# The written-out order of the first units and of the last stores in a fused HGRN2 and bilinear-FFN kernel

## The chip, the cores and the metric

The kernel runs on one core of a Trainium2 chip. The metric is the device time of one execution in microseconds (us). Three executions of the kernel before took 578.60, 579.79 and 579.91 us; the median is 579.79.

## The reference

The first stage is a gated linear attention (HGRN2 with outer products), the second a bilinear feed-forward network on its output:

```python
# q, k, v, f_logit: (B=4, H=8, S=768, D=48), fp32
f = 1.0 / (1.0 + np.exp(-f_logit))
for t in range(S):
    state = f[:, :, t, :, None] * state + np.einsum('bhd,bhe->bhde', k[:, :, t], v[:, :, t])
    y[:, :, t] = np.einsum('bhd,bhde->bhe', q[:, :, t], state)
x = y.transpose(0, 2, 1, 3).reshape(B * S, H * D)          # 3072 x 384
out = ((x @ w_a) * (x @ w_b)) @ w_out                      # 384 -> 1536 -> 384
```

The three weights are float64 in device memory and are turned into fp32 on the chip.

## The kernel before, in words

`by_quotients` is the main path. It cuts the attention into 16 units: unit u is one batch entry, one half of the sequence (384 tokens) and four heads. Two units give the 384 columns of x for a block of 384 tokens, so there are 8 blocks. Three sets of buffers hold the inputs of the units in turn. A unit goes through these stages, named as in the code:

- `front_parts`, in four parts of up to three steps. Part 0 is the sigmoid of the logits and two more steps on ScalarE (ACT). Part 1 on VectorE (DVE) holds two running products along the sequence (`scan_f`) and a third step, `hold`, which compares and counts for a test at the end. Part 2 restarts the products at the boundaries of small chunks and takes their inverse. Part 3 multiplies k (first step) and q (second step) by them.
- `turn` transposes k on TensorE (PE), `turned` copies the result (kT) out of PSUM on ACT, `scores` multiplies k and q within a chunk of 64 tokens (L426), `mask` applies the causal pattern on DVE (L443), `gains` forms the state products of v and kT (L506), `carried` sums the states on DVE.
- `within` multiplies the masked scores by v (L566), `across` the states by q (L592), both into the unit's PSUM bank. `y_of` copies it to SBUF on ACT (L610) and stores it to xT (L632).

The FFN of a block follows: `up` (L676 for the first block), `product`, `down`. Weights arrive in 12 pieces of 768 KB. `load_weights` issues the next piece on SyncE (SP), L275; `begin(n)` and `end(n)` emit the first and the last part of the conversion of the pieces up to n (half steps such as 2.5 emit half of a begin), on ACT, DVE and GpSimd (POOL).

For the first four units the order of all engines' work is written out by hand, as a list of calls that starts at L1202; each engine does its instructions in the order in which the list emits them. Later units are placed by a planner, whose rules stay as they are. The list has three calls of `keep_up` (L1190): products of the identity and a buffer of running products into an idle PSUM bank, which nobody reads. The names `idle[-1]` and `ps_f_68` stand for such a bank; the buffer, `products_of_f`, is part of the tile `groups`.

At the end a number (`bad`) that the kernel has computed decides over a branch. One arm computes everything again in another way; the other, short one does what the list `ending` holds. `down_thirds` (L981) is the last block's second FFN matmul by a scheme with few products: it makes sums of products in the PSUM banks v, u, r, t, and `c` holds the block's result, in three block rows of two halves. `add` and `add_steps` are DVE sums (L795), `store` is an output DMA (L1028). Every engine reads `bad` and goes over the branch (L142).

Of the kernel before, what the change touches and what calls it, by code (L numbers as in the profile page):

```python
# [22 lines left out]
BLK = 384  # L23
# [130 lines left out]
def by_quotients(ctx, tc, q, k, f_logit, v, moe_w_a, moe_w_b, moe_w_out, out, ident, weights, bad, ps_f):  # L154
# [64 lines left out]
    def load_unit(u, names="fkqv"):  # L219
        for do in loads_of(u, names):  # L220
            do()
# [40 lines left out]
    def load_weights(n=1):  # L262
        for _ in range(n):
            if len(raws) == len(todo):
                return
            dst, src, (k, m) = todo[len(raws)]
            raw = dst
            if src.dtype != FP32:

                if len(raws) in EARLY:  # L270
                    raw = groups[:, EARLY.index(len(raws))].bitcast(mybir.dt.uint64)
                else:
                    raw = next(raw_places)
                raw = raw[:, 0:k * m].rearrange("p (k m) -> p k m", k=k)
            nc.sync.dma_start(out=raw, in_=src)  # L275
            raws.append(raw)

    def begin(n):

        while 2 * n > begun[0] < 2 * len(todo):  # L280
            i, second = divmod(begun[0], 2)
            dst, src, shape = todo[i]
            if not second:
                going.append(
                    from_double(
                        nc, dst, raws[i], shape[0], next(blocks), bits[i % len(bits)], some, whole, shape[0] == NKT
                    )
                    if src.dtype != FP32 else iter(())
                )
            next(going[i], None)  # L290
            begun[0] += 1
# [126 lines left out]
    def scores(u):  # L418
        t = sets[u % NSET]
        qf, kf = halves(t["q"]), halves(t["k"])  # L420
        ps = pair_of(home(u))
        for n, c, o in each():
            for h in range(2):
                for p in range(2):
                    r = slice(R * h, R * h + D)
                    nc.tensor.matmul(  # L426
                        ps[h][SUB * p:SUB * p + SUB, o:o + SUB],
                        lhsT=kf[r, tokens(n, c, p)],
                        rhs=qf[r, tokens(n, c, p)],
                        start=True,  # L430
                        stop=True,
                    )

    def mask(u):

        if u == NQ - 1:

            at = raws4[:, 3 * PIECE:4 * PIECE].bitcast(FP32)[:, 0:2 * BLK].rearrange("s (h t) -> s h t", h=2)
        else:
            at = sb1.tile([128, 2, BLK], FP32, tag="at", name="at")  # L440
        to, x = (y.rearrange("s h (o t) -> s h o t", t=SUB) for y in (at, home(u)[:, :, 0:BLK]))
        tri = causal.unsqueeze(1).unsqueeze(1)
        nc.vector.tensor_tensor(to, x, tri.broadcast_to((128, 2, 2 * NC, SUB)), ALU.mult)  # L443
        live[u]["at"] = at
# [112 lines left out]
    def within(u):  # L557

        t, at = sets[u % NSET], live[u]["at"]
        ps = live[u]["y"] = pair_of(home(u) if u < 2 * NQ else ps_y)  # L560
        for n, c, o in each():
            for p in range(2):
                for h in range(2):
                    r = slice(SUB * p, SUB * p + SUB)
                    e = R * (p ^ h)
                    nc.tensor.matmul(  # L566
                        ps[p][e:e + D, o:o + SUB],
                        lhsT=t["v"][r, n, c, h * D:h * D + D],
                        rhs=at[r, h, o:o + SUB],
                        start=o == 0,  # L570
                        stop=True,
                        skip_group_check=True,
                    )
# [85 lines left out]
    def on(engine, load, due, do, *args, copied=False):  # L659
        return engine + COPIED * copied, load, beats[0] + due if due else 1 << 30, do, *args  # L660
# [325 lines left out]
    def down_thirds(blk, ending=None):  # L986
# [36 lines left out]
        def add(due, k, i, ps):  # L1023
            return on(DVE, 270, due, add_steps, c[:, k, i], c[:, k, i], ps, ALU.subtract if k == 1 else ALU.add)
# [61 lines left out]
        if ending is not None:  # L1086
            yield from times(v, "v6")
            ending.extend((
                (add_steps, c[:, 2, 0], u, c[:, 2, 0]), (store, 2), (write, c[:, 1, 0], v, -1), (store, 1, slice(0, 1)),
            ))  # L1090
            return
        yield add(5, 2, 0, u)
        yield on(SP, ISSUE, 0, store, 2)
        yield from times(v, "v6")
# [77 lines left out]
    with tc.manual_schedule():  # L1172
# [13 lines left out]
        def emit_all(steps):  # L1186
            for _, _, do, *args in steps:
                do(*args)

        def keep_up(n, to):  # L1190

            x = products_of_f[0][:, 0]
            for _ in range(n):
                nc.tensor.matmul(to[:, 0:BLK], lhsT=ident, rhs=x, start=True, stop=True)

        def y_of(u):
            for part in range(3):
# [1 line left out]
            stored(u)  # L1199


        for u in FIRST:  # L1202
            load_unit(u, "f")
        for u in FIRST:
            emit_all(parts[u][0])
        patterns()
        for u in FIRST:
            load_unit(u, "k")
            load_unit(u, "q")
            load_weights()  # L1210
            load_unit(u, "v")
        load_unit(2, "f")
        load_weights()
        load_unit(2, "k")
        load_unit(2, "q")
        for part in parts[0][1:]:
            emit_all(part)
        begin(1)
        keep_up(5, ps_f[idle[-1]])
        turn(0)  # L1220
        turned(0)
        scores(0)
        begin(2)
        gains(0)
        keep_up(5, ps_f[idle[-1]])
        for part in parts[1][1:]:
            emit_all(part)
# [12 lines left out]
        within(1)  # L1240
        gains(1, range(NC - 1, NC), range(1))
        load_weights()
        across(0)
        y_of(0)
        end(1)
        carried(1, range(1, NJ - 1))
        emit_all(parts[2][1])
        across(1)

        gains(1, range(NC - 1, NC), range(1, 2))  # L1250
        y_of(1)
        carried(0, range(NJ - 1, NJ))
        keep_up(2, ps_f[idle[-1]])
        begin(3)
        end(2)
        emit_all(parts[2][2])
# [7 lines left out]
        load_unit(3, "k")  # L1264
        load_unit(3, "q")
        up(0, 0, True)
        emit_all(parts[2][3])
        begin(4)
        emit_all(parts[3][0])
        end(3)  # L1270
        load_unit(3, "v")
        end(4)
# [2 lines left out]
        load_unit(4, "f")  # L1275
        up(0, 1)
        mask(2)
        product()
        for u in FIRST:
            hand_on(u)  # L1280
        turned(2)
        begin(5)
        emit_all(parts[3][1])
        within(2)
        gains(2)
        carried(2)
        up(0, 2)
        end(5)
        product()
        begin(6)  # L1290
        across(2)
        end(6)
        load_weights(2)
        y_of(2)
        emit_all(parts[3][2])
        product()
        up(0, 3)
        begin(7)
        emit_all(parts[3][3])
        product()  # L1300
        up(0, 4)
        begin(8)
        turn(3)
        scores(3)
        turned(3)
        end(8)
        mask(3)
        up(0, 5)
        product()
        begin(9)  # L1310
        within(3)
        gains(3)
# [1 line left out]
        carried(3)  # L1314
        product()
        up(0, 6)
        begin(10)
        across(3)
        end(10)
# [579 lines left out]
```

## Time and profile before

The table has the numbers of the profiled execution beside those of the runs.

| what | value |
|---|---|
| median of 3 runs | 579.79 us |
| the profiled execution's own time | 580.7 us |
| span of its instructions | 578.9 us |
| granted TensorE clock, mean | 0.998 of full speed |
| PE matmuls busy | 559.7 us (97%) |
| DVE busy | 440.3 us (76%) |
| ACT busy | 292.6 us (51%) |
| POOL busy | 92.3 us (16%) |
| data moved by DMA | 50.32 MB, mean 87 GB/s |

A row of the timeline gives the start in us, the duration in us, engine, line, operation, output and inputs, the shape (partitions x elements) and how many equal instructions are put together; in brackets stands the idle time ahead of it and what ended that. The trace shows each fp32 product of the program as two weight loads (PEld) and two matmuls (PE), a transposition as one of each, so the 24 score products of a unit appear as x48. In the chain of waits, "issue" is time in which an engine waited for nothing that the profile shows. In the DMA view q1 is the queue of the SP and ACT transfers, q8 and q14 bring instructions.

### The profile page before, as it was taken

What the parts mean: (1) busy time and instruction counts of PE and PEld (TensorE: products, weight loads), DVE (VectorE), ACT (ScalarE), POOL (GpSimd) and SP (SyncE); (2) the same over time, 40 slices, a digit from 0 to 9 for tenths busy, and PEclk for the clock granted to TensorE, in tenths of its full rate; (3) what the DMA queues carried; (4) which work ended last, traced back from release to release, by engine and by line L of the source; (5) the groups of instructions that cost most, each with busy time, mean ns of one, the idle gap of its engine ahead of it and who ended that gap; (6) DMA issues with size and microseconds to landing.
All of it is one profiled execution on the core that took longest, in us unless ns stands there. A gap on an engine that the chain in (4) does not pass through costs nothing.

```text
span 578.9 us, 13899 instructions
## 1 busy us (share of the span) xinstructions
PE 559.7 (97%) x5712; PEld 500.3 (86%) x5712; DVE 440.3 (76%) x817; ACT 292.6 (51%) x562; POOL 92.3 (16%) x77
## 2 busy tenths in 40 slices
PE   4789999999999999999999999999999999999996
PEld 2655655657999999999999999999999999999996
DVE  6888647798899877978689696988779655946691
ACT  7588777742324646254651666246561555234521
POOL 5466466630010401010010101010000000000000
PEclk9999999999999999999999999999999999999999
DMA  8789499060625940330440223410430300010001
GB/s 206 199 245 316 127 231 314 20 109 23 135 66 104 152 101 14 92 66 16 101 97 23 62 63 67 103 54 21 66 77 1 67 22 8 15 41 1 2 0 50
DMA packets 46571, 50.32 MB, mean 87 GB/s; under 512 B 16592, under 2 KB 40320, under 8 KB 46496
## 3 DMA queue, kind: packets, MB, share of 16 engines
q1 hardware_dynamic: 42528, 45.19, 31.5%
q0 software_dynamic: 3552, 3.69, 4.3%
q8 instruction: 47, 0.77, 0.5%
q10 hardware_dynamic: 416, 0.44, 0.2%
q14 instruction: 28, 0.23, 0.1%
HBM read 33.23 MB, written 4.72 MB: 66 GB/s over the span
## 4 chain that ended last, share of the span: by engine, by line
PE 91%; DVE 3%; ACT 2%; issue 2%; DMA 1%; SPq 0%; ACTq 0%; DVEq 0%
PE ps_f L803 39%; PE ps_f L1009 20%; PE ps_f L676 16%; PE ps_f L896 7%; PE ps_y L566 2%; PE ps_x L426 2%; PE ps_y L592 2%; PE ps_x L506 1%; DVE groups L346 1%; ACT groups L1546 1%; DMA f_in<-in_f_logit_dram 1%; ACT k_in L610 1%; DMA xT<-groups 0%; ACT sums L1546 0%; PE ps_x L455 0%
## 5 line engine op out<-in xcount | busy, mean ns | idle before, releaser
L1546 ACT COPY groups<-ps_f 128x384 f32<-128x384 f32 (+1 forms) x158 | 69.9, 443 | 115.7 <-PE ps_f L1009 48.0
L676 PE MATMUL ps_f<-xT,w_ba 128*128 128x384 f32 x288 | 96.4, 490 | 1.5 <-DMA xT<-groups 1.5
L676 PEld LDWEIGHTS ps_f<-xT,w_ba 128*128 128x128 f32 x288 | 53.6, 190 | 37.8 <-DMA xT<-groups 2.1
L1546 ACT COPY sums<-ps_f 128x384 f32<-128x384 f32 x120 | 57.6, 480 | 46.4 <-PE ps_f L803 33.7
L803 PE MATMUL ps_f<-xT,w_ba 128*128 128x192 f32 x384 | 79.0, 328 | 0.1
L803 PEld LDWEIGHTS ps_f<-xT,w_ba 128*128 128x128 f32 x384 | 64.4, 190 | 1.3 <-ACT groups L1546 0.7
L73 POOL TENSOR_SCALAR sums<-sums 128x768 f32<-128x768 f32 (+1 forms) x20 | 53.3, 2667 | 40.1 <-ACT sums L71 38.7
L342 POOL TENSOR_SCALAR inv<-inv 128x768 f32<-128x768 f32 x13 | 12.5, 959 | 274.9 <-ACT inv L336 250.3
L803 PE MATMUL ps_f<-groups,w_ba 128*128 128x192 f32 x288 | 56.0, 329 | 0.0
L803 PE MATMUL ps_f<-x_sums,raw 128*128 128x192 f32 x288 | 53.5, 330 | 0.3 <-DVE groups L795 0.3
L803 PEld LDWEIGHTS ps_f<-x_sums,raw 128*128 128x128 f32 x288 | 47.2, 190 | 2.4 <-ACT sums L1546 1.6
L803 PEld LDWEIGHTS ps_f<-groups,w_ba 128*128 128x128 f32 x288 | 47.8, 190 | 0.5
L795 DVE TENSOR_TENSOR groups<-groups 128x512 f32<-128x512 f32 (+2 forms) x52 | 42.4, 818 | 5.5 <-ACT groups L1546 3.5
L795 DVE TENSOR_TENSOR sums<-ps_f,sums 128x384 f32<-128x384 f32 x60 | 33.1, 553 | 15.6 <-PE ps_f L803 13.6
L795 DVE TENSOR_TENSOR sums<-sums,groups 128x768 f32<-128x768 f32 (+1 forms) x39 | 34.0, 872 | 13.9 <-ACT groups L1546 13.4
L795 DVE TENSOR_TENSOR groups<-ps_f,groups 128x384 f32<-128x384 f32 x60 | 33.1, 553 | 9.3 <-PE ps_f L803 7.6
L803 PE MATMUL ps_f<-xT,raw 128*128 128x192 f32 x192 | 39.5, 328 | 0.6 <-ACT groups L1546 0.6
L803 PE MATMUL ps_f<-x_sums,w_ba 128*128 128x192 f32 x192 | 39.2, 327 | 0.0
L1009 PE MATMUL ps_f<-spare,groups 128*128 128x192 f32 x192 | 35.2, 327 | 0.0
L803 PEld LDWEIGHTS ps_f<-xT,raw 128*128 128x128 f32 x192 | 32.3, 190 | 1.4 <-ACT groups L1546 1.2
L1009 PE MATMUL ps_f<-w_out,groups 128*128 128x192 f32 x192 | 33.2, 326 | 0.0
L803 PEld LDWEIGHTS ps_f<-x_sums,w_ba 128*128 128x128 f32 x192 | 32.5, 190 | 0.1
(197 smaller groups left out, 987.0 us busy)
## 6 DMA issues: line engine op xcount, KB each, us to landing
k_in<-in_k_dram SPq DMA_DIRECT2D x32, 144.0 KB, 3.7
q_in<-in_q_dram SPq DMA_DIRECT2D x32, 144.0 KB, 4.0
v_in<-in_v_dram SPq DMA_DIRECT2D x16, 288.0 KB, 5.2
raw<-in_moe_w_out_dram SPq DMA_DIRECT2D x6, 768.0 KB, 7.8
f_in<-in_f_logit_dram SPq DMA_DIRECT2D x28, 144.0 KB, 3.0
out_dram<-groups SPq DMA_DIRECT2D x17, 192.0 KB, 1.9
raw<-in_moe_w_b_dram SPq DMA_DIRECT2D x4, 768.0 KB, 8.9
raw<-in_moe_w_a_dram SPq DMA_DIRECT2D x4, 768.0 KB, 8.3
```

The lines of the kernel that those rows point to most:

```text
L73: nc.gpsimd.tensor_scalar(h, h, HI_MIN, HI_MAX, ALU.max, ALU.min)
L342: nc.gpsimd.tensor_scalar(inv, inv, EXP_K, 1.0, ALU.mult, ALU.add)
L346: nc.vector.tensor_tensor_scan(F[:, c], F[:, c], none, math.exp(MIDDLE), ALU.mult, ALU.add)
L426: nc.tensor.matmul(ps[h][SUB * p:SUB * p + SUB, o:o + SUB], lhsT=kf[r, tokens(n, c, p)], rhs=qf[r, tokens(n, c, p)], start=True, stop=True,)
L566: nc.tensor.matmul(ps[p][e:e + D, o:o + SUB], lhsT=t["v"][r, n, c, h * D:h * D + D], rhs=at[r, h, o:o + SUB], start=o == 0, stop=True, ski ...
L592: nc.tensor.matmul(ps[p][e:e + D, o:o + SUB], lhsT=st[j][r, n], rhs=qf[r, tokens(n, c, p)], start=False, stop=True, skip_group_check=True,)
L676: nc.tensor.matmul(ps[nm][:, 0:BLK], lhsT=w[:, kt, ft * 128:ft * 128 + 128], rhs=xT[blk][:, kt], start=kt == 0, stop=kt == NKT - 1,)
L795: nc.vector.tensor_tensor(to, x, y, op)
L803: nc.tensor.matmul(ps[:, g], lhsT=sums_of_w[name][:, g, 128 * j:128 * j + 128], rhs=sums_of_x[blk][name], start=start and g == 0, stop=Tru ...
L896: nc.tensor.matmul(to, lhsT=x[:, i], rhs=w[:, i], start=start and i == 0, stop=i == HFT - 1, skip_group_check=True,)
L1009: nc.tensor.matmul(to, lhsT=x[:, i], rhs=w[:, i], start=start and i == 0, stop=i == NJ3 - 1, skip_group_check=True)
L1546: do(*args)
```

## The change

Four things are changed in the written-out order of the first units, and one at the end.

1. `keep_up` takes a width and a number of rows. The first call, 5 products of 128x384, becomes 17 of 128x128; the second, 5 of 128x384, becomes 10 of 128x128 and 47 of 64x64 on 64 rows; the third goes from 2 to 3 products of 128x384.
2. PE does `scores(1)` ahead of `within(0)`. DVE does `mask(0)` ahead of the q step of unit 1, `hold` behind the steps that begin the products again, and `hold` of unit 2 ahead of that unit's sigmoid and scans (it then compares the loaded logits).
3. The masked scores of unit 1, `at`, lie in x_sums and no longer in the fourth quarter of the raw buffer, into which the fourth weight piece is loaded.
4. Conversions are emitted in halves at other places, unit 2's sigmoid comes behind part of a piece's conversion, and k of unit 3 is loaded ahead of its f. Many lines only write a former loop out step by step (`step(u, part, i)`).
5. The last block's sum with t2 (`c[:, 0, 1]`), the sum with `second` and the stores of block row 0 and of one half of block row 1 leave the main path, where ACT issued the stores, and go into the list `ending` of the short arm, on DVE and SP. `second` then lies in w_ba.

The diff, cut to what matters:

```diff
-            at = raws4[:, 3 * PIECE:4 * PIECE].bitcast(FP32)[:, 0:2 * BLK].rearrange("s (h t) -> s h t", h=2)
+            at = x_sums[:, 0:2 * BLK].rearrange("s (h t) -> s h t", h=2)
...
-        first, second = (last[:, BLK * n:BLK * n + BLK].rearrange("p (n m) -> p n m", n=2) for n in range(2))
+        places = last[:, 0:BLK], last[:, BLK:2 * BLK] if ending is None else w_ba[:, 0, 0, 3 * BLK:4 * BLK]
+        first, second = (x.rearrange("p (n m) -> p n m", n=2) for x in places)
...
+        if ending is not None:
+            yield from times(u, "u5")
+            yield from times(v, "v6")
+            ending.extend((
+                (add_steps, c[:, 0, 1], c[:, 0, 1], t), (add_steps, c[:, 0], c[:, 0], second), (store, 0),
+                (store, 1, slice(1, 2)), (add_steps, c[:, 2, 0], u, c[:, 2, 0]), (store, 2),
+                (write, c[:, 1, 0], v, -1), (store, 1, slice(0, 1)),
+            ))
+            return
         yield add(8, 0, 1, t)
         yield on(DVE, 480, 0, add_steps, c[:, 0], c[:, 0], second, copied=True)
-        if ending is not None:
-            yield on(ACT, ISSUE, 0, store, 1, slice(1, 2), nc.scalar)
-            yield on(ACT, ISSUE, 0, store, 0, slice(0, 2), nc.scalar)
-        else:
-            yield on(SP, ISSUE, 0, store, 0)
+        yield on(SP, ISSUE, 0, store, 0)
...
-        def keep_up(n, to):
+        def keep_up(n, width=BLK, rows=128):
+            to = ps_f[idle[-1]]
             x = products_of_f[0][:, 0]
             for _ in range(n):
-                nc.tensor.matmul(to[:, 0:BLK], lhsT=ident, rhs=x, start=True, stop=True)
+                nc.tensor.matmul(to[0:rows, 0:width], lhsT=ident[0:rows, 0:rows], rhs=x[0:rows, 0:width], start=True, stop=True)
...
         begin(1)
-        keep_up(5, ps_f[idle[-1]])
+        keep_up(17, 128)
         turn(0)
         turned(0)
         scores(0)
+        begin(1.5)
         begin(2)
         gains(0)
-        keep_up(5, ps_f[idle[-1]])
-        for part in parts[1][1:]:
-            emit_all(part)
+        keep_up(10, 128)
+        step(1, 1, 0)
+        keep_up(47, 64, 64)
...
+        step(1, 3, 0)
         turn(1)
         turned(1)
         mask(0)
+        step(1, 3, 1)
+        scores(1)
+        step(2, 1, 2)
         within(0)
-        scores(1)
-        emit_all(parts[2][0])
         begin(2.5)
+        carried(0, range(NJ - 1))
         gains(1, range(NC - 1))
-        carried(0, range(NJ - 1))
+        step(2, 0, 0)
...
         mask(1)
         carried(1, range(1))
         within(1)
         gains(1, range(NC - 1, NC), range(1))
+        across(0)
         load_weights()
-        across(0)
         y_of(0)
...
-        keep_up(2, ps_f[idle[-1]])
+        keep_up(3)
         begin(3)
```

On PE, the place is between unit 0's state products and unit 1's. ps_f_68 holds the unread products, k_in_89 and q_in_88 are unit 1's k and q, v_in_87 is unit 0's v and v_in_91 unit 1's:

```order
-L1194 MATMUL ps_f_68<-groups,ident 128x384 x5
+L1195 MATMUL ps_f_68<-groups,ident 128x128 x10
+L1195 MATMUL ps_f_68<-groups,ident 64x64 x47
 L455 MATMUL ps_f_67<-ident,k_in_89 128x112 x3
 L455 MATMUL ps_f_68<-ident,k_in_89 128x112 x3
+L426 MATMUL ps_y<-q_in_88,k_in_89 64x64 x24
 L566 MATMUL ps_x<-at,v_in_87 48x64 x24
-L426 MATMUL ps_y<-q_in_88,k_in_89 64x64 x24
 L506 MATMUL ps_f_67<-v_in_91,kT 48x48 x2
 L506 MATMUL ps_f_68<-v_in_91,kT 48x48 x2
```

Five unread products have become 57 narrower ones, and the scores of unit 1 have moved ahead of within(0).

On SP, the place is the fourth weight piece, the second of w_a, between the loads of unit 2's q (q_in_92) and the first stores to xT. The names in brackets are the semaphores that a transfer waits for:

```order
 L234 DMA q_in_92<-in_q_dram 48x2x384 [waits DMAHW5_49,Pool_49]
 L234 DMA q_in_92<-in_q_dram 48x2x384 [waits DMAHW6_49]
-L275 DMA raw<-in_moe_w_a_dram 128x3x256 [waits DMAHW7_49,DVE_49,PE_49]
+L275 DMA raw<-in_moe_w_a_dram 128x3x256 [waits DMAHW7_49]
 L632 DMA xT<-groups 48x384 [waits DMAHW0_49,Activation_49]
 L632 DMA xT<-groups 32x384 [waits DMAHW1_49]
```

The piece stands at the same place in the queue, but no longer waits for DVE and PE.

On DVE, at the end of the program, ahead of the branch:

```order
 L795 TENSOR_TENSOR w_ba<-w_ba,ps_f_67 128x192
 L1159 TENSOR_LOAD bad
-L795 TENSOR_TENSOR w_ba<-w_ba,ps_f_66 128x192
-L795 TENSOR_TENSOR w_ba<-w_ba,groups 128x384
 L142 COMPARE_AND_BRANCH
```

and in the short arm:

```order
 L142 UNCONDITIONAL_BRANCH
+L795 TENSOR_TENSOR w_ba<-w_ba,ps_f_66 128x192
+L795 TENSOR_TENSOR w_ba<-w_ba 128x384
 L795 TENSOR_TENSOR w_ba<-ps_f_67,w_ba 128x192
 L142 UNCONDITIONAL_BRANCH
```

The two sums have moved from ahead of the branch into the arm, ahead of the sum that stood there before.

More of the change, by code (lines that the diff above doesn't have):

```diff
@@ L1188, in emit_all, with step @@
                 do(*args)
-        def keep_up(n, to):
+        def keep_up(n, width=BLK, rows=128):
+            to = ps_f[idle[-1]]
             x = products_of_f[0][:, 0]
             for _ in range(n):
-                nc.tensor.matmul(to[:, 0:BLK], lhsT=ident, rhs=x, start=True, stop=True)
+                nc.tensor.matmul(to[0:rows, 0:width], lhsT=ident[0:rows, 0:rows], rhs=x[0:rows, 0:width], start=True, stop=True)
+        def step(u, part, *which):
+            for i in which:
+                emit_all(parts[u][part][i:i + 1])
         def y_of(u):
@@ L1199, in y_of @@
             stored(u)
[L1202 to L1205, printed above, removed]
-        patterns()
[L1207 to L1211, printed above, removed]
+        load_unit(0, "f")
+        load_unit(1, "f")
+        step(0, 0, 0)
+        step(0, 0, 1)
+        step(0, 0, 2)
+        step(1, 0, 0)
+        step(1, 0, 1)
+        step(1, 0, 2)
+        patterns()
+        load_unit(0, "k")
+        load_unit(0, "q")
+        load_weights()
+        load_unit(0, "v")
+        load_unit(1, "k")
+        load_unit(1, "q")
+        load_weights()
+        load_unit(1, "v")
         load_unit(2, "f")
@@ L1215, in by_quotients @@
         load_unit(2, "q")
-        for part in parts[0][1:]:
-            emit_all(part)
+        step(0, 1, 0)
+        step(0, 1, 1)
+        step(0, 2, 0)
+        step(0, 2, 1)
+        step(0, 1, 2)
+        step(0, 2, 2)
+        step(0, 3, 0)
+        step(0, 3, 1)
+        begin(0.5)
         begin(1)
-        keep_up(5, ps_f[idle[-1]])
+        keep_up(17, 128)
         turn(0)
@@ L1222, in by_quotients @@
         scores(0)
+        begin(1.5)
         begin(2)
         gains(0)
-        keep_up(5, ps_f[idle[-1]])
-        for part in parts[1][1:]:
-            emit_all(part)
+        keep_up(10, 128)
+        step(1, 1, 0)
+        keep_up(47, 64, 64)
+        step(1, 1, 1)
+        step(1, 2, 0)
+        step(1, 1, 2)
+        step(1, 2, 1)
+        step(1, 2, 2)
+        step(1, 3, 0)
         turn(1)
@@ L1277, in by_quotients @@
         mask(2)
+        hand_on(0)
         product()
-        for u in FIRST:
-            hand_on(u)
+        step(3, 1, 0)
+        hand_on(1)
         turned(2)
+        begin(4.5)
         begin(5)
-        emit_all(parts[3][1])
+        step(3, 1, 1)
+        step(3, 1, 2)
         within(2)
@@ L1289, in by_quotients @@
         product()
+        begin(5.5)
         begin(6)
@@ L1294, in by_quotients @@
         y_of(2)
-        emit_all(parts[3][2])
+        step(3, 2, 0)
+        step(3, 2, 1)
+        step(3, 2, 2)
         product()
         up(0, 3)
+        begin(6.5)
         begin(7)
-        emit_all(parts[3][3])
+        step(3, 3, 0)
+        step(3, 3, 1)
         product()
         up(0, 4)
+        begin(7.5)
         begin(8)
@@ L1305, in by_quotients @@
         turned(3)
+        end(7)
         end(8)
```

31 lines of the change are left out of this document (18 added, 13 removed).

## The prediction

> **What bounds the kernel now.** I read the page first, then the chain of waits, then the timeline of the first 30 us on all engines, the DMA view of short stretches of it, and the timeline of the last 10 us.
>
> ```profile
> span 578.9 us, 13899 instructions
> PE 559.7 (97%) x5712; PEld 500.3 (86%) x5712; DVE 440.3 (76%) x817; ACT 292.6 (51%) x562; POOL 92.3 (16%) x77
> ...
> q8 instruction: 47, 0.77, 0.5%
> ```
>
> PE is the bound: it lacks 19 us of the span. An edit that adds no PE work in the long middle can only act on the start and on the end. The third line matters later: 47 packets of 0.77 MB in all, 16.4 KB each, bring instructions.
>
> The chain of waits names what ends last in the start:
>
> ```profile
> 21.43 1.09 issue
> 22.52 0.34 PE ps_y L426 x3
> ...
> 25.79 0.28 issue
> 26.07 0.27 PE ps_x L592 x3
> ...
> 28.56 2.60 DMA xT<-groups
> ...
> 31.29 1.53 PE ps_f L676 x4
> ...
> 47.04 0.86 issue
> ```
>
> Three times PE stops for nothing that the profile shows, and each time inside a row of equal instructions: after 45 of 48 scores of unit 1, after 37 of 40 products of across(0), and in unit 2. From 31.29 the FFN keeps PE busy, so what moves across(0), whose result goes to xT and starts the FFN, moves the end of the program.
>
> The timeline gives the counts and durations between the stops (start, duration, operation, count):
>
> ```profile
> 7.28 6.25 PE L1194 MATMUL ps_f<-groups,ident 128*128 128x384 f32 x10 [7.28 <-DVE groups L346]
> 13.36 0.74 PE L455 MATMUL ps_f<-ident,k_in 112*128 112x112 f32 x6
> 13.85 0.78 ACT L462 COPY kT<-ps_f 128x336 f32<-128x336 f32 x2 [0.91 <-PE ps_f L455]
> 14.03 0.93 PE L426 MATMUL ps_x<-q_in,k_in 48*64 48x64 f32 x48
> 14.78 0.72 PE L506 MATMUL ps_f<-v_in,kT 64*48 64x48 f32 x48
> 15.43 3.49 PE L1194 MATMUL ps_f<-groups,ident 128*128 128x384 f32 x10
> 17.05 1.02 DVE L374 TENSOR_TENSOR k_in<-k_in,spare 128x768 f32<-128x768 f32 x1
> 17.99 0.95 DVE L374 TENSOR_TENSOR q_in<-q_in,groups 128x768 f32<-128x768 f32 x1
> 18.75 0.74 PE L455 MATMUL ps_f<-ident,k_in 112*128 112x112 f32 x6
> 19.86 0.89 PE L566 MATMUL ps_x<-at,v_in 64*48 64x64 f32 x48 [0.36 <-DVE at L443]
> 20.57 0.87 PE L426 MATMUL ps_y<-q_in,k_in 48*64 48x64 f32 x45
> ...
> 22.64 0.57 PE L506 MATMUL ps_f<-v_in,kT 64*48 64x48 f32 x32
> 23.90 0.89 PE L566 MATMUL ps_y<-raw,v_in 64*48 64x64 f32 x48 [0.68 <-DVE raw L443]
> 24.61 0.30 PE L506 MATMUL ps_f<-v_in,kT 64*48 64x48 f32 x6
> 24.70 0.99 PEld L592 LDWEIGHTS ps_x<-q_in,st 48*48 48x48 f32 x37
> 24.74 0.21 PE L506 MATMUL ps_f<-v_in,kT 64*48 64x48 f32 x2
> ```
>
> Each counted product is a weight load and a matmul, a pair; an unread product is two pairs (five give x10). Up to the first stop PE does 10+6+48+48+10+6+48+45 = 221 pairs, from there to the second 3+32+48+8+37 = 128. I read the stops as ends of pieces of 128 pairs, one q8 packet each: 128 pairs are 256 instructions, and 16.4 KB over 256 is 64 bytes. So boundaries lie at pairs 93 (P1, in the state products of unit 0), 221 (P2), 349 (P3) and 477 (P4). The DMA view shows when the packets moved; the shares are of 16 engines over 0.1 us, from 19.5 and from 23.7 us:
>
> ```profile
> q1 hardware_dynamic: 20, 0.03, 103.9%
> q8 instruction: 1, 0.02, 86.8%
> ```
>
> ```profile
> q8 instruction: 1, 0.02, 57.4%
> ```
>
> P2's packet took 0.868 x 1.6 = 1.39 us from 19.5, P3's 0.92 us from 23.7. PE goes on 1.6 and 1.4 us after a packet's end. P3's packet starts 1.2 us after PE came into P2 (22.52), so I take it that a piece is asked for when PE enters the one before it. The shortest step from piece to piece is then 26.07 - 22.52 = **3.55 us**. P2, asked for about 14.9, was far slower: its packet started near 19.5, among q1's transfers, which SP had issued:
>
> ```profile
> 13.38 0.39 SPq L275 DMA_DIRECT2D raw<-in_moe_w_b_dram  x1
> 14.10 0.79 SPq L234 DMA_DIRECT2D k_in<-in_k_dram  x2
> 15.14 1.20 SPq L234 DMA_DIRECT2D q_in<-in_q_dram  x2
> 24.87 0.38 SPq L275 DMA_DIRECT2D raw<-in_moe_w_a_dram  x1
> ```
>
> [...]
>
> **The change, part by part.**
>
> *Unread products.* Five products become 17 of 128 columns, 34 pairs in place of 10; the second five become 10 of 128 columns (20 pairs) and 47 of 64x64 (94 pairs). That is 34+20+94-10-10 = 128 pairs more before across(0), one whole piece. The first group has 34x128 = 4352 columns against 3840, 512 more at 6.25/3840 = 1.63 ns cold, or at 0.91 (3.49/3840) after the clock has risen: +0.5 to +0.8, I take 0.7. The kT copies then end at 15.3 in place of 14.63, and unit 0's state products, with P1 in them, run from there to 16.1.
>
> The price of a 64-column pair is in no row. Scores with 64 columns cost 0.93/48 = 19 ns, in four quadrants of PE; a transposition of 112 columns 0.74/6 = 123 ns; by columns 349 x 64/384 = 58. I take 54 to 58, since these products are of the kind of the 384-column ones, with bounds 19 and 123. Then PE is at pair 221 at 16.1 + 20x0.11 + 65x0.054 = 21.8. In the trace of before it was there at 21.43. A later stop at the same instruction number gains nothing: the packet decides.
>
> *P2.* It is asked for up to 0.7 later, among the same transfers: 22.52 + 0.7 = 23.2 (22.0 if it slips ahead of q's second half; 25 if it goes behind the weight piece as well). PE waits 1.4 us, in unread products. Left before P3 are 29 of these (1.6 us), the transpositions (0.74), scores(1) (0.87) and within(0) (0.71, from its start to the next row's), to 27.1.
>
> *The fourth weight piece early.* mask(1) writes x_sums in place of raws4[3], and the piece of w_a no longer waits for DVE and PE: SP issues it behind q, at about 16.5 in place of 24.87. Its 768 KB are needed much later, so the early arrival itself brings nothing. It keeps the DMA engines full to about 25, an estimate from the w_b piece, k and q, which were issued from 13.38 and still had q1 at 104% near 19.5. P3's packet, asked for at 23.2, would start at 24.9 in place of 24.4: P3 at 27.3 (26.75 without it). On the other side the stores to xT no longer stand behind this piece: -0.3 (0 to -0.6, of the 2.60 us that the transfer took in the chain).
>
> *P4.* From P3 to P4 lie state products, within(1), more state products and all but the last 4 of across(0)'s 40 products, about 2.5 us of PE work, less than the step of 3.55. P4 comes at 27.3 + 3.55 = 30.85 and across(0) ends at 30.95. Before, it ended at 26.07 + 0.27 = 26.34. That is **+4.6 us**, and the piece that was added is the whole of it. If P2 came at 22.0 and P3 and P4 at the shortest step, P4 would still be at 29.1: +2.8.
>
> *Orders on DVE, ACT, POOL, SP.* mask(0) ahead of q, hold behind the scans' beginnings, unit 2's hold on the loaded logits ahead of its scans, the sigmoid of unit 2 behind the conversion of a weight piece, k ahead of f for unit 3: the same instructions. DVE has k of unit 1 at 18.07; now q follows at 17.99 for 0.95, and the mask behind it until PE starts within(0) at 19.86. With the mask ahead, at about the same 0.95, q is there at 19.97 in place of 18.94. Covered by the wait for P2; if that goes, this 1.0 is the next thing late (a rival below). The third group of unread products, 2 to 3, costs 0.7 in a place where PE waits for xT: nothing.
>
> *The third stop.* One piece more moves no boundary against the instructions behind across(0), since exactly 128 pairs were added. 0, with bounds of the stop's own 0.86 to both sides.
>
> *The end.* Two sums of DVE and two stores move from ahead of the branch into its arm.
>
> ```profile
> 568.48 0.35 DVE L795 TENSOR_TENSOR w_ba<-w_ba,ps_f 128x192 f32<-128x192 f32 x1 [2.99 <-PE ps_f L1009]
> 569.79 2.61 ACTq L1028 DMA_DIRECT2D out_dram<-w_ba  x2
> 571.47 0.56 DVE L795 TENSOR_TENSOR w_ba<-w_ba,groups 128x384 f32<-128x384 f32 x1
> 572.11 1.46 PE L1009 MATMUL ps_f<-groups 128*128 128x192 f32 x8
> 574.52 0.36 DVE L795 TENSOR_TENSOR w_ba<-ps_f,w_ba 128x192 f32<-128x192 f32 x1 [2.49 <-PEq L142]
> 574.90 1.10 SPq L1028 DMA_DIRECT2D out_dram<-w_ba  x2
> 575.15 0.33 ACT L715 ACTIVATE w_ba<-ps_f 128x192 f32<-128x192 f32 x1 [5.06 <-DVE w_ba L795]
> ```
>
> DVE needs 2.49 us over the branch, ACT about 2.75 (575.15 after its last issue, 572.40). After the change both reach the branch earlier: DVE is done at 568.83, ACT has no stores. If each engine goes over it by itself, DVE is in the arm by 572.4, adds t2 and second to 573.45, and four stores of SP, 0.6 apart, follow; the last begins at 575.25 in place of 575.50: -0.25. If the arm opens only with PE, at 574.5, the same row of work ends 1.85 later. I take -0.25, since DVE's and ACT's rows each measure from their own last work.
>
> *Sum:* +4.6 - 0.3 + 0 - 0.25 = +4.05 us against the profiled execution of 580.7 (span 578.9): 584.75. The median of the runs, 579.79, lies 0.91 below that execution, so I forecast **583.8**.
>
> **The rivals.** About 0.3% (1.7 us) is what a measurement of this kernel can tell from no change.
>
> (B) *The 64-column pairs are dear.* Above 73 ns the unread products themselves reach pair 221 later than P2. At 100 ns they reach it at 24.8 and end at 27.7; P3 is entered at 30.0, P4 comes at 33.55: +7.2 at across(0), and 586.4. For it: the 123 ns of the transpositions. Against it: 349 ns per 384 columns leaves little for a fixed part.
>
> (C) *The pieces come in time, and the time is less.* If P2 is asked for before k and q fill the queues, or a piece further ahead than I read, no stop is left, and DVE's q at 19.97 decides: scores(1) to 20.9, within(0) 21.7, state products 22.2, within(1) 23.1, across(0) 24.0 in place of 26.34. With the end that is -2.6: **577.2**, faster. It decides where P2's packet moves before about 16 us. For it: a boundary that falls among unread products is where a stop costs least, and P1 is crossed after 5 state products in place of 29. Against it: P2's packet near 19.5 shows 4.6 us of waiting, and the transfers ahead of it are the same. [...]
>
> (D) *Late, but less.* P2 at 22.0, P3 at 25.5 untouched by the weight piece, and P4's boundary some pairs further on, behind across(0): the counts rest on records, of which a few can be missing. across(0) ends near 27.4, +1.05; with the other terms +0.5, or 580.3, no change.
>
> **How the numbers follow.** Forecast 0.55 (its own range 581.2, from P2 at 22.0 with shortest steps and a little off the other terms, to 586.0, with P2 at 25 or the dear end), B 0.10, C 0.22, D 0.13. So faster 0.22, same 0.13, slower 0.65. Leaving out B alone and the outer tails of the forecast keeps 8 in 10 safely: 576.5 to 586.2.
>
> **What would show it.** In the profile after: a stop without a releaser among the 64x64 products until 22 to 24 us; a second near the end of within(0); a third in the last few products of across(0), near 30; three q8 packets between 19 and 30, each 1.0 to 1.7 us after PE went on. The w_a piece issued near 16.5. The FFN's first L676 row near 35.5 in place of 31.29. If q8's packets come before 16 us, or PE crosses the 64x64 products without a stop, the forecast is wrong and C holds; if the 64x64 rows take over 100 ns a pair, B. At the end, the DVE row of the arm near 572.4 shows the one reading, at 574.5 the other.

## The result, and the profile after

The changed kernel takes 584.65 us (median of 6 runs, 583.74 to 586.35) against 579.32 for the kernel before (6 runs on the same chip, 578.60 to 579.91). The ratio is 1.0096, with a 95% interval of 1.0079 to 1.0112: 5.6 us slower (4.6 to 6.5). The profiled execution after took 586.35 us with a span of 584.5, 5.6 above the span before. Single executions of one kernel differ by 1 to 5 us here, and other sets of the kernel before had medians of 579.86 to 580.32; so below a change in us is always the ratio within one set times 580, and positions in time come from the profiles.

The page of after has 260 PE instructions more and one q8 packet more:

```profile
span 584.5 us, 14158 instructions
...
PE 565.9 (97%) x5842; PEld 510.1 (87%) x5842; DVE 440.7 (75%) x817; ACT 292.5 (50%) x562; POOL 92.0 (16%) x77
...
q8 instruction: 48, 0.79, 0.6%
```

PE in the timeline of after:

```profile
7.26 5.94 PE L1195 MATMUL ps_f<-groups,ident 128*128 128x128 f32 x34 [7.26 <-DVE groups L346]
13.04 0.74 PE L455 MATMUL ps_f<-ident,k_in 112*128 112x112 f32 x6
...
15.11 6.43 PE L1195 MATMUL ps_f<-groups,ident 128*128 128x128 f32 x85
21.87 1.85 PE L1195 MATMUL ps_f<-groups,ident 64*64 64x64 f32 x29 [0.33 <-issue]
...
25.12 0.84 PE L566 MATMUL ps_x<-at,v_in 64*48 64x64 f32 x44
27.94 0.32 PE L566 MATMUL ps_x<-at,v_in 64*48 64x64 f32 x4 [1.98 <-issue]
...
28.58 1.50 PE L566 MATMUL ps_y<-x_sums,v_in 64*48 64x64 f32 x47
...
30.16 1.87 PE L592 MATMUL ps_x<-q_in,st 48*48 48x64 f32 x37
...
36.63 1.89 PE L676 MATMUL ps_f<-xT,w_ba 128*128 128x384 f32 x5 [1.39 <-DMA xT<-groups]
```

The first stop falls 85 pairs into the second group, 20 wide ones and 65 of the 64x64 products, with 29 left: that is pair 221. The second falls 4 pairs ahead of the end of within(0). The FFN starts at 36.63 in place of 31.29. These three rows of DMA views, 0.2 us each from 19.2, 25.4 and 29.0 us, show the packets of the next pieces (34.1% of 16 engines over 0.2 us is 1.09 us):

```profile
q8 instruction: 1, 0.02, 34.1%
```

```profile
q8 instruction: 1, 0.02, 34.8%
```

```profile
q8 instruction: 1, 0.02, 36.4%
```

PE goes on 1.6 and 1.4 us after the ends of the first two. SP issues the fourth weight piece at 17.57 (24.87 before), and P3's packet starts only at 25.4, 3.5 us after PE entered P2:

```profile
17.57 0.39 SPq L275 DMA_DIRECT2D raw<-in_moe_w_a_dram  x1
```

After the second stop there is no third one. Instead, PE runs at half the clock for 3.4 us, as the table of stretches shows (the column ahead of the DMA share is the granted clock; its 0.66 and 0.63 put the fall at 28.3 and the rise at 31.7):

```profile
28.00:29.00 1.00, 1.00 (x54) 1.00 (x57) 0.12 (x1) 0.48 (x1) 0.92 (x2) 0.66 0.00 0
29.00:30.00 1.00, 1.00 (x46) 1.00 (x40) 0.39 (x2) 0.00 (x0) 0.57 (x1) 0.50 0.07 16
30.00:31.00 1.00, 1.00 (x28) 1.00 (x24) 0.52 (x3) 0.00 (x0) 0.00 (x0) 0.50 0.00 0
31.00:32.00 1.00, 1.00 (x36) 0.93 (x34) 0.96 (x5) 0.00 (x0) 0.00 (x0) 0.63 0.03 8
```

P4's packet was there at 30.3, and so P4, by the same 1.4 to 1.6 us, at about 31.8, just as the slow PE came to it. Not every execution had this stretch: 3.4 us at half take 0.003 off the mean clock, and two of the six executions have a mean of 0.999, with 583.74 and 584.53 us. The profiled one is the slowest of the six. From the FFN's start to the end of PE's last product are 542.20 us, against 542.28 before: the middle is unchanged in sum. The end of after:

```profile
577.37 1.46 PE L1010 MATMUL ps_f<-groups 128*128 128x192 f32 x8
577.40 0.35 DVE L795 TENSOR_TENSOR w_ba<-w_ba,ps_f 128x192 f32<-128x192 f32 x1 [3.31 <-issue]
...
578.45 1.83 SPq L1029 DMA_DIRECT2D out_dram<-w_ba  x4
578.93 0.33 ACT L715 ACTIVATE w_ba<-ps_f 128x192 f32<-128x192 f32 x1 [3.64 <-PE ps_f L1010]
```

DVE is in the arm while PE still works, so the arm does not open with PE. From the last product's end (578.83) to the end of the span are 5.67 us, against 5.33 before.

### The profile page after: what moved, and what is told of

Same layout as the page of the kernel before. It is cut to its first block, busy times and chain, and to the rows that moved or that the text cites. A ratio compares the mean times of both kernels' runs of the same rounds, so it can differ in the third digit from the quotient of the medians.

```text
span 584.5 us, 14158 instructions
## 1 busy us (share of the span) xinstructions
PE 565.9 (97%) x5842; PEld 510.1 (87%) x5842; DVE 440.7 (75%) x817; ACT 292.5 (50%) x562; POOL 92.0 (16%) x77
## 4 chain that ended last, share of the span: by engine, by line
PE 89%; DMA 4%; ACT 2%; DVE 2%; issue 1%; SPq 1%; DVEq 0%; ACTq 0%
PE ps_f L803 39%; PE ps_f L1010 20%; PE ps_f L676 13%; PE ps_f L896 7%; PE ps_f L1195 2%; PE ps_y L566 2%; PE ps_x L426 2%; DMA raw<-in_moe_w_b_dram 2%; PE ps_y L592 2%; PE ps_x L506 1%; DMA groups<-in_moe_w_a_dram 1%; ACT groups L1591 1%; DMA f_in<-in_f_logit_dram 1%; ACT k_in L610 1%; ACT sums L1591 0%
```

## The experiments

The theory is that of the prediction: pieces of 128 pairs, each asked for when PE enters the one before, with at least some 3.6 us from piece to piece and more when transfers are ahead. Against it stand: the early weight piece alone, the orders alone, and a price per instruction wherever it stands.

**The change without its added instructions.**

```diff
-        keep_up(17, 128)
+        keep_up(5)
...
-        keep_up(10, 128)
+        keep_up(5)
         step(1, 1, 0)
-        keep_up(47, 64, 64)
```

> The kernel after, but its first two groups of unread products are again 5 and 5 of 128x384; the early weight piece, the orders and the end stay. Theory (instruction pieces): pair 221 lies 3 pairs ahead of the end of within(0), so that PE stops there until about 22 to 22.5 us; pair 349 lies 3 pairs ahead of the end of across(0), whose packet stands behind the early weight piece and starts near 25.4, so that PE goes on at 27.9. across(0) ends near 28.2 in place of 32.1 after and 26.3 before: about 581 us. Rival 1 (the early weight piece and not the added instructions makes the loss): as after, 584.5. Rival 2 (the added instructions are everything): 579.3, as before, or less by the orders' gain.

Ratio 1.0024 (1.0005 to 1.0044): +1.4 us. The timeline has the stops where the count puts them, at 4 pairs from the end of within(0) and after 38 of 40 products of across(0):

```profile
21.72 0.32 PE L566 MATMUL ps_x<-at,v_in 64*48 64x64 f32 x4 [0.50 <-issue]
...
27.20 0.26 PE L592 MATMUL ps_x<-q_in,st 48*48 48x64 f32 x2 [3.09 <-issue]
```

The second, 3.09 us, I read as the wait for the packet behind the weight piece. So of the 5.6 us, some 4 go with the 128 added pairs.

**The change with the weight piece late.**

```diff
-            at = x_sums[:, 0:2 * BLK].rearrange("s (h t) -> s h t", h=2)
+            at = raws4[:, 3 * PIECE:4 * PIECE].bitcast(FP32)[:, 0:2 * BLK].rearrange("s (h t) -> s h t", h=2)
```

> The kernel after, but mask(1) writes the raw buffer again, so that the fourth weight piece waits for DVE and PE as before. Theory (instruction pieces): P2 still at 21.9 us in the 64x64 products; P3's packet starts near 23.1 and PE is past pair 349 at about 25.9 without a stop over 0.3 us and without the half clock; P4 is asked for at 25.9 and comes at about 29.4, so that across(0) ends near 29.6 in place of 32.1: about 582.5 us. Rival 1 (the early weight piece makes the loss): 579.5. Rival 2 (it costs nothing): 584.5, as after.

Ratio 1.0071 (1.0044 to 1.0099): +4.1 us. The trace has one stop without a releaser ahead of the FFN, at P4, and a clock of 1.00 throughout:

```profile
28.72 0.26 PE L592 MATMUL ps_x<-q_in,st 48*48 48x64 f32 x2 [1.30 <-issue]
...
33.56 4.21 PE L676 MATMUL ps_f<-xT,w_ba 128*128 128x384 f32 x12 [1.37 <-DMA xT<-groups]
```

Without the early weight piece the FFN starts 2.3 us later than before. The early weight piece adds 3.07 us to the FFN's start on top of it (36.63 against 33.56) and 1.5 to the time (1.0096 against 1.0071, with intervals that overlap). The first of these two traces is the slowest of its six executions, though, and the second the fastest of its six. The stops are where they were expected, but by the time alone, 584.25 us, the run lies nearer to the rival that the early weight piece costs nothing (584.5) than to the 582.5 expected.

**The weight piece early in the kernel before** (the same line, the other way).

> The kernel before with one line changed: mask(1) writes x_sums, so that the fourth weight piece is issued behind q of unit 2, near 17.5 us. Theory: P2 as before near 22.5, P3's packet only behind the weight piece's transfers near 25.4, so that PE stops in across(0) until 27 to 28 in place of 26.07; the stores to xT gain 0.4. In all +0.5 to +1.5: 579.8 to 580.8. Rival 1 (it alone makes the loss): 584.5. Rival 2 (only the stores gain): 578.9.

Ratio 1.0013 (0.9995 to 1.0030), which the runs cannot tell from no change. The timeline shows the mechanism all the same:

```profile
27.51 0.26 PE L592 MATMUL ps_x<-q_in,st 48*48 48x64 f32 x2 [3.02 <-issue]
...
32.36 4.16 PE L676 MATMUL ps_f<-xT,w_ba 128*128 128x384 f32 x12 [0.44 <-DMA xT<-groups]
```

The stop that was 0.28 us is 3.02. Part of it came back, since PE's later stop in unit 2 (0.86 before) is not there.

**The added instructions in the kernel before** (`keep_up` and its first two groups as in the change, nothing else).

> The kernel before, but its first two groups of unread products are those of after (17 of 128x128; 10 of 128x128 and 47 of 64x64), 128 pairs more. Theory (instruction pieces): P2 falls into the 64x64 products (29 pairs left) at about 22, P3 comes 3.55 later at the earliest, 25.5, and P4, 4 pairs ahead of the end of across(0), 3.55 after that, 29.1: across(0) ends 2.8 to 3.3 later than before: 582.1 to 582.8. Rival 1 (instructions cost only their own time; PE has 1 us of idle time there): 579.3 to 580. Rival 2 (the piece alone is the whole loss): 584.5.

Ratio 1.0057 (1.0035 to 1.0080): +3.3 us. With the 1.4 of the run that lacks only these instructions it makes 4.7 of the 5.6, within the intervals. The added products end at 22.7, and PE's one stop without a releaser ahead of the FFN is the one at P4:

```profile
14.42 8.31 PE L1195 MATMUL ps_f<-groups,ident 128*128 128x128 f32 x114
...
28.81 0.32 PE L592 MATMUL ps_x<-q_in,st 48*48 48x64 f32 x4 [0.55 <-issue]
...
33.94 4.48 PE L676 MATMUL ps_f<-xT,w_ba 128*128 128x384 f32 x12 [1.13 <-DMA xT<-groups]
```

Here the stop is short, 0.55 us, because the 114 pairs take 8.31 us themselves, and PE crosses P2 among them without a stop. So in this run the products' own time and the late piece carry nearly the same price, and it does not tell them apart. The new orders with the new end have no run of their own: the change with the weight piece late differs from this run by them and by one product more in the third group, and 1.0071 against 1.0057 is within the intervals.

**Half of the added instructions in the kernel before** (17 of 128x128, then 10 of 128x128 and 15 of 64x64).

> The kernel before with 17 of 128x128, then 10 of 128x128 and 15 of 64x64 as unread products: 64 pairs more than before, half of those of the change. Theory (pieces of 128 pairs, a step of 3.6 us): pair 221 lies 29 pairs into within(0), pair 349 lies 29 pairs into within(1), and pair 477 beyond across(0), so that only two late pieces stand ahead of across(0)'s end, as before. A stop in within(0) until about 21.7, one in within(1) until about 25.4, across(0) ends near 27.0 in place of 26.3: +0.7 us, 580.5. Rival (each added instruction costs the same): half of the 3.3 to 4 us of the full piece, +1.8, 581.6, and no stop within within(1).

Ratio 1.0012 (0.9995 to 1.0029): +0.7 us, with half of the full piece's price (1.6) at the edge of the interval. The timeline has both stops at the predicted pair:

```profile
20.67 0.65 PE L566 MATMUL ps_x<-at,v_in 64*48 64x64 f32 x29
22.38 0.48 PE L566 MATMUL ps_x<-at,v_in 64*48 64x64 f32 x18 [1.06 <-issue]
...
25.72 0.48 PE L566 MATMUL ps_y<-raw,v_in 64*48 64x64 f32 x18 [0.39 <-issue]
```

29 pairs into within(0) and 28 or 29 into within(1). So in this run, too, the boundaries are at the pairs that the count gives, 221 and 349. Whether the price goes by pieces or by instructions this run does not decide: half of the full price lies just inside its interval, and in the traces its FFN starts 1.1 us later than before, against 2.7 with the full piece.

**The end alone, in the kernel before.**

> The kernel before with the change at the end alone: the sum with t2, the sum with second and the stores of block rows 0 and 1b go into the short arm. The two profiles with the new end so far have 5.46 us from the end of PE's last product to the end of the span, against 5.33 before. Theory (the sums and stores are hidden, but four stores in a row replace two): +0.1 us in the profile, from 0 to +0.4, nothing that the runs can tell: 579.9. My term of the prediction said -0.25: 579.6. Rival (the arm opens only with PE): +1.8, 581.7.

Ratio 1.0003 (0.9988 to 1.0018): nothing that can be told. In the trace the span ends 6.1 us after PE's last product (570.15 + 1.46 to 577.7), 0.8 more than before:

```profile
571.85 2.55 SPq L1029 DMA_DIRECT2D out_dram<-w_ba  x4
```

The start of this kernel is that of the kernel before, and so its trace shows how far single traces differ. P2's packet starts ahead of 18.5 us in place of 19.5, PE has no stop at P2, and the FFN starts at 30.36 in place of 31.29:

```profile
30.36 4.48 PE L676 MATMUL ps_f<-xT,w_ba 128*128 128x384 f32 x12 [1.87 <-DMA xT<-groups]
```

A difference of up to 0.9 us between the positions in two traces, above and below, therefore shows little by itself.

**Fewer pairs in the kernel before: 4 and 4 in place of 5 and 5.**

> The kernel before, with 4 and 4 unread products in place of 5 and 5 and nothing else: 4 pairs fewer. Theory: the two stops of 1.09 us and 0.28 us move from 3 pairs ahead of the end of scores(1) and across(0) to the pair behind them: mask(1), which waits for the last scores, runs 1 us earlier, PE waits for P2 until 22.5 in the state products, and across(0) ends before its stop, 0.5 to 1 us earlier than before: 579.0 to 579.5, and the stops in the trace stand 1 pair behind these rows. Rival (the boundaries are elsewhere or not at fixed counts): the stops stay 3 pairs ahead of the ends, and no change, 579.9.

Ratio 0.9992 (0.9976 to 1.0007): no change. The expected 0.5 to 1 us did not come. All of the stops without a releaser ahead of the FFN are gone, across(0) ends at 24.6 in place of 26.3, but the FFN gives the time back:

```profile
23.47 1.11 PE L592 MATMUL ps_x<-q_in,st 48*48 48x64 f32 x39
...
30.72 5.80 PE L676 MATMUL ps_f<-xT,w_ba 128*128 128x384 f32 x12 [2.23 <-DMA xT<-groups]
```

PE waited 2.23 us for xT, and then the first 12 products took 5.80 us in place of 4.37. The granted clock in that trace is 0.50 from 32 to 35 us.

**The same, with 4 in place of 2 in the third group.**

```diff
-        keep_up(2, ps_f[idle[-1]])
+        keep_up(4, ps_f[idle[-1]])
```

> The kernel before with 4 and 4 unread products and 4 in place of 2 in the third group, ahead of the FFN. With 2, PE was idle for 2.23 us ahead of the FFN, and the first 12 FFN products took 5.80 us in place of 4.1 to 4.4. Theory (after more than about 1.9 us of idle time the clock is granted at half for some 3 us): idle time under 1.2 us, the first 12 products in 4.1 to 4.4 us, the FFN's start as in that run, so 1 to 1.5 us less in the profile; in the runs 579.0 to 579.5. Rival (the slow products came from another cause, such as transfers): still 5.5 us or more, no change, 579.9. Rival 2 (the products are late themselves and hold up the FFN): FFN's start 0.5 to 1 us later.

Ratio 0.9978 (0.9963 to 0.9994): 1.3 us faster than the kernel before by the ratio (the medians are 579.11 and 580.11), and the only run here that is faster clear of the noise:

```profile
26.76 2.85 PE L1194 MATMUL ps_f<-groups,ident 128*128 128x384 f32 x8 [0.65 <-DVE st_end L537]
29.87 4.15 PE L676 MATMUL ps_f<-xT,w_ba 128*128 128x384 f32 x12 [0.26 <-DMA xT<-groups]
```

The clocks of the single executions agree. With 2 products, 4 of 12 executions have a mean clock of 0.998 or more, which leaves no room for 3.4 us at half, and take 578.63 to 579.63 us; with 4 it is 9 of 12, and they take 578.18 to 579.42. The intervals of the two runs overlap, so their times alone do not show what the two products bring.

**The change with fewer pairs** (weight piece late, 4 and 4 in the first two groups).

> The kernel after, with the weight piece late again (raw buffer) and 4 and 4 unread products of 128x384: 4 pairs fewer than before ahead of across(0). Theory: pair 221 then lies 1 pair behind within(0), pair 349 1 pair behind across(0). PE waits once, until about 21.9, and does state products, within(1) and across(0) from one piece: across(0) ends near 24.5 in place of 26.34 before. across(1) waits for the next piece until about 25.5 and ends near 26.4 in place of 27.1. The FFN starts 0.7 to 1.9 us earlier than before: 578.0 to 579.2. Rival 1 (the order on PE and DVE costs as much as it gains, since the boundaries are not what counts): 579.9. Rival 2 (fewer unread products let the clock fall, so that all stages run at half rate for some us): 581 or more.

Ratio 1.0007 (0.9993 to 1.0021): the gain was missed. The boundaries went as expected and across(0) ended at 23.9, but ACT, the next in the row, was late:

```profile
21.35 0.57 PE L506 MATMUL ps_f<-v_in,kT 64*48 64x48 f32 x32 [0.18 <-issue]
...
22.82 1.11 PE L592 MATMUL ps_x<-q_in,st 48*48 48x64 f32 x39
```

```profile
22.00 0.93 ACT L71 ACTIVATE sums<-raw 128x768 f32<-128x768 f32 x1 [2.84 <-DMA raw<-in_moe_w_b_dram]
...
25.68 1.45 ACT L610 COPY groups<-ps_x 48x384 f32<-48x384 f32 x3
```

A weight piece that lands at 22.0 holds ACT, and its conversion and unit 2's sigmoid stand ahead of the copy, 1.75 us after across(0). The FFN starts 1.1 us earlier than in the trace of before, but only 0.2 us earlier than in the trace of the run with the new end:

```profile
30.16 4.23 PE L676 MATMUL ps_f<-xT,w_ba 128*128 128x384 f32 x12 [1.90 <-DMA xT<-groups]
```

**The new PE order, and the conversion behind the copies** (the kernel before with 4 and 4, mask(0) ahead of q, scores(1) ahead of within(0), and `begin(2.5)` moved behind both `y_of`).

> The kernel before with 4 and 4 unread products, mask(0) ahead of q and scores(1) ahead of within(0) as in the change, the first half of the third piece's conversion (2.9 us of ACT from the weight piece's arrival) behind the copies of both units, and 3 products in the third group. In the run with fewer pairs on the new order, across(0) ended at 23.9 us, but ACT copied it only at 25.7, behind that conversion and unit 2's sigmoid. Theory (boundaries no longer bind, ACT does): copies at 23.9 to 24.2, FFN from about 28.6 in place of 30.2 to 31.3: 1 to 2 us less than before, 578.3 to 579.2. Rival 1 (the conversion is then late for the FFN): PE waits for DVE at w_ba L83 near 40 to 58 us for as long as was gained: 580. Rival 2 (the stores to xT or the clock take it back): FFN from 30 us on, or the first FFN products at 1.5 times their duration: 580.

Ratio 1.0039 (1.0024 to 1.0054): 2.3 us slower. The trace shows rival 1. The FFN starts at 29.55, 1.7 us earlier than before, but the conversion's POOL step is now late (22.68 before), SP's next loads with it (33.47 us in the chain of waits, 31.83 before), and PE waits 1.09 us for unit 2's v and 0.82 for weights:

```profile
29.88 2.76 POOL L73 TENSOR_SCALAR sums<-sums 128x768 f32<-128x768 f32 x1 [1.51 <-ACT sums L71]
```

```profile
40.97 0.89 PE L566 MATMUL ps_x<-at,v_in 64*48 64x64 f32 x48 [1.09 <-DMA v_in<-in_v_dram]
...
57.62 4.44 PE L676 MATMUL ps_f<-xT,w_ba 128*128 128x384 f32 x12 [0.82 <-DVE w_ba L83]
```

So the gain is gone there: the row that starts at 57.62 starts at 57.86 in the trace of before, and the spans are 579.1 and 578.9. That is no loss of 2.3 us. The profiled execution is the fastest of its twelve, 1.2 us below their median, and where the others lose the rest stays open.

## Why the prediction was right, and where its sizes were not

The forecast was 583.8 and the time is 584.65; in the profiles, +4.05 stands against +5.6. The mechanism holds as far as the boundaries go: the boundary at pair 221 was in its place to a pair or two wherever a trace shows it, in kernels with 4 fewer, 64 more and 128 more pairs, and the share of the added instructions was found alone at +3.3 (2.0 to 4.6). Several terms were off, and that the sum came within 0.9 us is in part luck: P2 came earlier than forecast, while the weight piece and the clock cost more.

The prediction calls the added piece the whole of the loss at across(0), and that is not shown, because no run separates the late pieces from the products' own time. In the trace of after, the second group holds PE from 15.11 to 23.64, 5.2 us longer than before, while the stops without a releaser ahead of the FFN sum to 2.31 us against 1.37. PE came to pair 221 only 0.33 us ahead of its piece, so the products alone would have brought it there nearly as late. With the weight piece late PE crosses P2 and P3 without a stop, and only the 1.30 us at P4 are a wait for a piece. The same number of cheaper products would decide it; there is no such run.

- *First group, +0.7.* It ended at 13.04, earlier than before (13.36). In the traces with the old 10 pairs this group took 5.0 to 6.25 us, with 34 pairs 5.4 to 6.6; the execution decides more than the width. In the trace of after the pairs start 0.21 us apart up to 11.2 us and 0.11 behind, in that of before 0.64 apart up to 12.5 us and 0.32 behind. The traces' records of the granted clock begin, at 1.00, where the distances halve, at 11.26 us after and at 12.89 before. So the fast pairs came more than 1 us earlier in the trace of after, and that hides the price of the columns. No record stands ahead of these; that the slow pairs are those of a lower clock is my reading.
- *64-column pair, 54 to 58 ns.* 29 took 1.85 us, 64 ns. Rival B falls.
- *P2 at 23.2.* It came at 21.87: its packet started at 19.2, not later than before, and the early weight piece did not push it back. 1.3 too late in the forecast.
- *P3 at 27.3.* It came at 27.94, although P2 was early. The weight piece was the mis-sized term: I gave it 0.55 us, and it cost 2.5, from the shortest step of 3.55 to 6.07. The run without it shows P3 at no cost at all.
- *P4 stops PE until 30.85.* No stop: in the profiled execution PE at half the clock came to it late by itself. I had no term for the clock. within(1) took 1.28 us and across(0) 1.65 in the chain of waits, where within(1) had taken 0.89, and across(0) ended at 32.1, 1.1 after the forecast.
- *xT, -0.3.* The transfer took 2.21 in place of 2.60 us: -0.4.
- *Third stop, 0.* The 0.86 us is gone, and PE waits 0.8 us for converted weights (DVE, L83) instead, as in the change without its added instructions and the change with fewer pairs (0.82 us each), though not in the change with the weight piece late. It sums to 0.
- *End, -0.25.* It was +0.34. The row on which I relied (each engine goes over the branch by itself) held: DVE was in the arm at 577.40 with PE at work until 578.83. It needed 3.31 us over the branch, though, in place of the 2.49 that I had read. And the last store, though issued 0.8 us earlier against PE's end, completed 0.3 us later. Beside the stores the DMA view of the 0.2 us from 580.2 has a packet of instructions; that it is the next piece behind the branch and delayed the last rows is my reading and was not tested. The kernel before has such a packet too, from 574.7 to 575.7, but there it ends before the data of the last two stores start.

```profile
q1 hardware_dynamic: 30, 0.03, 50.2%
q8 instruction: 1, 0.02, 43.0%
```

Rival C (pieces in time) needed P2's packet ahead of 16 us. It came at 19.5 before and at 19.2 after, between 18.5 and 19.5 in three more traces, and ahead of 18.5 in that of the new end; with the boundaries put off by 4 pairs, though, its DVE-bound path showed: across(0) at 23.9 against the 24.0 that I had worked out, and ACT then late. Rival D's P2 near 22.0 came true, and the rest of it did not.

Where PE was busy for long enough until it came to a boundary, no stop was seen there: none at P4 with the half clock, and none at P2 and P3 with the weight piece late. At full speed with a weight piece ahead a crossing cost 1.98 us after, 3.02 in the kernel before with the early weight piece and 3.09 in the change without its added instructions.

## What to carry to other kernels

Where a profile has a stop with no releaser inside a row of equal instructions, count the instructions between such stops and look at when the instruction queue's packets move: here cheap instructions put into idle time still used up a piece (the added instructions alone cost 3.3 us), and an early load that nobody needed yet made a stop of 0.28 us one of 3.02. When such a stop is taken away, look at once for what is late next (here ACT's copy) and for idle time after which the clock falls (1.98 to 3.09 us here); the version that won here (1.3 us) moved 4 pairs of unread products from the first two groups to the one right ahead of the FFN.

## What the runs showed of the hardware

- A piece is 256 PE instructions in these traces: the counted pairs between the first two stops before are 128, and a packet of the instruction queue has 16.4 KB. That it is asked for when PE enters the one before it is inferred from three traces, in which a packet started about 1 us after PE had gone on into the piece before it: at 23.7 after 22.52 before, at 29.2 after 27.94 with the change, and with half of the added instructions in the quarters of a microsecond from 23.25 and 26.75, after 22.38 and 25.72. It was not always so soon: before, the next packet starts at 28.4, 2.4 us after 26.07, and with the new end alone in the quarter from 27.0, at least 1.8 us after 25.17. Up to P4 a packet started about 3.5 to 5 us after the one before it, and 6.2 us with the early weight piece between them (at 19.2 and 25.4 with the change); the packet itself takes 0.9 to 1.5 us. P2's packet, among unit 2's loads, started between 18.5 and 19.5 in five traces and ahead of 18.5 in that of the new end. With 768 KB of weights ahead, PE came from one piece to the next in 6.07 us after the change.
- PE slowed after idle times of 2 to 3 us in four traces. With the change, behind 1.98 us, the granted clock is 0.50 from 28.3 to 31.7, beginning 0.4 us after PE had gone on. With fewer pairs in the kernel before, behind 2.23 us, it is 0.97 from 31 to 32 and 0.50 from there to 35, beginning 1.2 us after. Behind the stops of 3.09 us (the change without its added instructions) and 3.02 us (the kernel before with the early weight piece) equal unread products were slow: three of 128x384 took 3.83 us against 2.20 with the weight piece late, and two took 2.49 against 1.56 before. Behind 1.87 us (the new end) and 1.90 us (the change with fewer pairs) the first 12 FFN products took 4.48 and 4.23 us, against 5.80 behind the 2.23. What else counts, and what sets the moment and the length of the fall, is not shown.
